# Storing attention's rows: 32 whole rows per transfer from all 128 partitions instead of quarter rows from 32 partitions

## The chip, the core and the metric

The kernel runs on one core of one Trainium2 chip. The metric is device time in microseconds (us) of one execution. The kernel before took 713.63 us, the median of three runs (708.15, 713.63 and 713.73 us).

## The reference

The computation is an attention block whose output feeds a mixture of experts. Eight batches have eight heads each, 576 positions and 64 values per head.

```python
# attention: a coarse one over means of 4 positions, plus a local one within 3 positions
out_d = sm_attn(q_d, k_d, v_d)               # q, k, v averaged in groups of 4
out_up = np.repeat(out_d, factor, axis=2)
scores = np.where(np.abs(pos[:, None] - pos[None, :]) < factor, scale * q @ k.T, -1e9)
attn_out = out_up + softmax(scores) @ v
# rows for the experts: 4608 tokens x 512 values (8 heads x 64)
x = attn_out.transpose(0, 2, 1, 3).reshape(B * S, H * D)
logits = x @ w_gate + modality_bias[modality_id]
e_idx = argmax(logits); gate_w = softmax(logits)[e_idx]
out[mask] = gate_w * (relu(x[mask] @ w1[e]) @ w2[e])     # for each of 8 experts
```

All tensors are float32. The result has 4608 rows of 512 values.

## The kernel before

The kernel has two stages that share one instruction stream per engine. In the **attention stage** the work goes in 32 steps called pairs: a pair is two heads of one batch that lie 64 partitions apart (`tpq` to `avl`, lines 254 to 447). Four pairs make a batch. `Attention.X` (L449) adds the coarse and the local part and writes the batch's tile `X` with the 512 values of a token down four groups of 128 partitions and the tokens along the free dimension.

The **router** (`Router`, L463) works batch by batch on `X`: it computes the gate's logits (`lg` to `gt`), the place of each token in its expert's list (`pr`, `pl`), and writes the lists to the DRAM tensor `tab` with an indirect DMA from GpSimd (`scatter`, L600). Two more steps bring the tokens' rows to DRAM, so that the experts can gather them:

- `R` (L580) transposes 128 tokens at a time on VectorE, in blocks of 32 by 32. After it, partition 32 a + j of tile `R` holds, for block i of 32 tokens, the 128 values with number 128 a to 128 a + 127 of token 32 i + j. These 128 values (512 bytes) lie side by side, as do the blocks i of one partition. One tile `R` takes two transposes, so 256 tokens in 8 blocks, or 128 tokens where a batch has an odd number of tiles.
- `store` (L590) copies one such tile to the DRAM tensor `xs`, which has one row of 512 values (2 KB) per token. This is what the change touches.

A batch has 576 tokens, so two batches fill nine tiles of 128: even batches handle four tiles in two stores, odd batches five tiles in three stores.

The order of the instructions is written out by hand. `PHASE` (L55) gives each step its due time, counted in pairs; `build` makes a list of calls with those times, sorts it, and issues them in that order under a manual schedule (L1115 to L1132). The stores `W0`, `W1` and `W2` are due 9.1, 11.1 and 8.5 pairs after the first pair of their batch. All plain DMAs are issued by SyncE (SP), and so stand in one queue in that order: the loads of q and k (`load_qk`, L221, three buffers each, due about four and a half pairs ahead of use), the loads of v (`load_v`, L233, two buffers), the stores, the lists of the first two units of expert work (`entries`, L826), and the weights (`wload`, L788, four buffers).

GpSimd has its own queue, in which steps of attention (`halves`, `whole`, `nl`, `nd`) stand with three kinds of work for the experts that are interleaved into the last batches: the scatter of the lists, the gather of rows for the first two units (`gather`, L844, the indirect DMA of L858, which reads `xs` and needs the unit's list `tg`), and the rounding of the first weights (`wsplit`, L800, L815 and L821), which waits for the weight load `raw`.

The **expert stage** begins inside the last pairs. A unit of work is up to 512 tokens of one expert; each product is made of three matmuls on rounded parts (`compute`, L888, line 906; `second`, L939, line 954). The first two units take tokens of the first four batches alone, so their rows can be gathered while attention goes on. The last batch's steps are issued in the stretch where the stages meet (L1140 to L1154): its row tiles go out by `R` and `store`, the last one through a tile named `o`.

Of the kernel before, what the change touches and what calls it, by code (L numbers as in the profile page):

```python
# [462 lines left out]
class Router:  # L463
# [126 lines left out]
    def store(s, b, t):  # L590

        n = min(2, s.t["G", b] - 2 * t)
        if n > 0:
            r0 = 128 * (s.t["t0", b] + 2 * t)
            R = s.t.pop(("R", b, t))
            for a in range(4):
                s.nc.sync.dma_start(s.xs[r0 : r0 + 128 * n, 128 * a : 128 * a + 128].rearrange("(i j) x -> j i x", j=32),
                                    R[32 * a : 32 * a + 32, : 4 * n].rearrange("p i k c -> p i (k c)"))

    def scatter(s, t0, t1):  # L600
        nc, C = s.nc, s.C
# [659 lines left out]
```

## Time and profile before

| | |
|---|---|
| median of three runs | 713.63 us (708.15 to 713.73) |
| the profiled execution, its own time | 717.73 us |
| its span, first to last instruction | 716.0 us |
| mean granted TensorE clock | 0.974 |
| attention stage | to about 275 us of the span |
| expert stage | from about 273 us to the end |
| stores of rows (L597) | 80 DMAs, issued from 77.8 to 285.3 us |

Busy time, idle time and waits come from the one profiled execution, and times in it count from the span's start. PE is TensorE's matmuls, PEld its weight loads, DVE is VectorE, ACT is ScalarE, POOL is GpSimd, and SP is SyncE, which issues the plain DMAs (SPq). A row of a timeline gives start, length, engine, line, operation, output and inputs, how many instructions were merged, and in brackets the idle time before the first one with what ended it. The "DMA share" is the mean busy share of the core's 16 DMA engines. A "packet" is one piece moved by one of them.

### The profile page before, as it was taken

Reading aid. Unit: us, or ns where it says so; the run is one execution under the profiler, and the core shown is the slowest. Engines: PE = TensorE matmul, PEld = TensorE weight load, DVE = VectorE, ACT = ScalarE, POOL = GpSimd, SP = SyncE. Lnnn points to the kernel's source line nnn. Section 1 sums busy time; section 2 is a strip of 40 time slices with the busy share of each in tenths; the row PEclk is TensorE's granted clock in tenths of the full one; section 3 lists DMA queues with packets and bytes.
Section 4 is the critical chain, followed back from the end, with each engine's and each line's share of the span. In section 5 each row is a group of like instructions: output and inputs, shape, how many; then the busy total and the mean of one; then the engine's idle time right before and its main releaser. Section 6 shows DMA issues by size and latency. Waiting matters only on the chain. (4 is left out here: it accounts for less than half of the span.)

```text
span 716.0 us, 19629 instructions
## 1 busy us (share of the span) xinstructions
PE 661.5 (92%) x7659; PEld 530.3 (74%) x7659; DVE 380.6 (53%) x877; ACT 359.1 (50%) x804; POOL 274.0 (38%) x366
## 2 busy tenths in 40 slices
PE   7889999998987689899999999999999999999894
PEld 4667676766765566787888888888888888889793
DVE  3678687797857585845732435224342343426610
ACT  4678777876855473634442344324443243425610
POOL 6746665856647658155030220401204012210211
PEclk9899999999998999999999999999999999999998
DMA  9799886997979767649562652535614345245600
GB/s 180 149 183 180 157 184 145 152 197 146 167 143 197 138 173 153 185 160 316 145 186 78 162 191 67 168 118 148 206 54 127 144 133 176 62 130 174 206 21 29
DMA packets 179584, 107.94 MB, mean 151 GB/s; under 512 B 139452, under 2 KB 157922, under 8 KB 179490
## 3 DMA queue, kind: packets, MB, share of 16 engines
q1 hardware_dynamic: 172274, 87.49, 52.7%
q0 software_dynamic: 7216, 19.18, 8.2%
q8 instruction: 61, 1.00, 0.7%
q14 instruction: 33, 0.27, 0.1%
HBM read 87.39 MB, written 19.51 MB: 149 GB/s over the span
## 5 line engine op out<-in xcount | busy, mean ns | idle before, releaser
L821 DVE TENSOR_TENSOR wlo<-raw,whi 128x1024 fp32r<-128x1024 f32 x73 | 87.6, 1224 | 87.0 <-ACT whi L815 66.6
L965 POOL DMA_INDIRECT out_dram<-o,tg x33 | 37.0, 1122 | 233.7 <-ACT o L957 179.7
L911 DVE SCALAR_TENSOR_TENSOR hl<-l,hh 128x512 fp32r<-128x512 f32 x72 | 49.4, 689 | 103.5 <-ACT hh L910 101.4
L954 PE MATMUL l<-whi,hh 128*128 128x512 f32 x256 | 100.5, 396 | 2.5 <-ACT hh L935 2.5
L954 PE MATMUL l<-whi,hl 128*128 128x512 f32 x256 | 99.8, 390 | 0.0
L954 PE MATMUL l<-wlo,hh 128*128 128x512 f32 x256 | 99.7, 390 | 0.0
L906 PE MATMUL l<-xh,whi 128*128 128x512 f32 (+1 forms) x256 | 95.7, 377 | 3.3 <-DVE hl L911 1.8
L910 ACT ACTIVATE hh<-l 128x512 fp32r<-128x512 f32 x72 | 42.8, 597 | 110.0 <-PE l L906 109.0
L906 PE MATMUL l<-xh,wlo 128*128 128x512 f32 (+1 forms) x256 | 94.8, 370 | 0.0
L906 PE MATMUL l<-xl,whi 128*128 128x512 f32 (+1 forms) x256 | 94.8, 370 | 0.0
L815 ACT CAST whi<-raw 128x1024 fp32r<-128x1024 f32 x70 | 71.5, 1050 | 31.3 <-DMA raw<-in_moe_w_dram 17.0
L957 ACT ACTIVATE o<-l,tg 128x512 f32<-128x512 f32 x37 | 25.3, 687 | 99.1 <-PE l L954 71.1
L906 PEld LDWEIGHTS l<-xh,whi 128*128 128x128 f32 x256 | 48.5, 190 | 12.8 <-DVE hl L911 2.1
L407 ACT COPY Pw<-lt 32x288 f32<-32x288 f32 x128 | 54.6, 427 | 6.6 <-issue 3.4
L954 PEld LDWEIGHTS l<-whi,hh 128*128 128x128 f32 x256 | 48.2, 188 | 12.2 <-ACT hh L935 2.7
L954 PEld LDWEIGHTS l<-wlo,hh 128*128 128x128 f32 x256 | 48.1, 188 | 10.1
L954 PEld LDWEIGHTS l<-whi,hl 128*128 128x128 f32 x256 | 48.3, 189 | 9.5
L337 PE MATMUL sc<-kT,qT 64*24 64x32 f32 x3072 | 45.4, 195 | 10.5 <-issue 9.6
L906 PEld LDWEIGHTS l<-xh,wlo 128*128 128x128 f32 x256 | 48.2, 188 | 8.3
L906 PEld LDWEIGHTS l<-xl,whi 128*128 128x128 f32 x256 | 48.3, 189 | 8.1 <-issue 0.2
L337 PEld LDWEIGHTS sc<-kT,qT 64*24 64x24 f32 x3072 | 35.2, 101 | 24.5 <-issue 20.2
L391 POOL TENSOR_TENSOR le<-le,zr 128x384 f32<-128x384 f32 x32 | 26.7, 835 | 63.9 <-DVE zr L387 56.4
(244 smaller groups left out, 1283.2 us busy)
## 6 DMA issues: line engine op xcount, KB each, us to landing
raw<-in_moe_w_dram SPq DMA_DIRECT2D x176, 128.0 KB
raw<-in_moe_w_dram SPq DMA_DIRECT2D x44, 512.0 KB
vw<-in_v_dram SPq DMA_DIRECT2D x53, 192.0 KB
qt<-in_q_dram SPq DMA_DIRECT2D x30, 288.0 KB
kt<-in_k_dram SPq DMA_DIRECT2D x30, 288.0 KB
xs<-R SPq DMA_DIRECT2D x64, 128.0 KB
vw<-in_v_dram SPq DMA_DIRECT2D x15, 96.0 KB
xs<-R SPq DMA_DIRECT2D x12, 64.0 KB
```

The costliest lines, as they stand in the source:

```text
L337: s.nc.tensor.matmul(p[32 * j : 32 * j + SUB, i, :], qT[r, q0 : q0 + SUB], kT[r, q0 : q0 + WIN], start=False, stop=(i == NB - 1), skip_gro ...
L391: s.nc.gpsimd.tensor_tensor(e, e, z[:, : 2 * NB].unsqueeze(2).broadcast_to([128, 2 * NB, WIN]), op=ALU.mult)
L407: s.nc.scalar.copy(s.Pw[n % NPW][r, :, j, :SUB], s.t["lt", n][r, :, :SUB])
L815: (nc.gpsimd.tensor_copy if turn <= 4 else nc.scalar.copy)(hi, raw)
L821: (nc.gpsimd if turn == 4 else nc.vector).tensor_tensor(lo, raw, hi.bitcast(F32), op=ALU.subtract)
L906: nc.tensor.matmul(p[:, f % n, :], a[:, fs], x[:, k, :N], start=(k == 0 and i == 0), stop=(k == 3 and i == 2))
L910: nc.scalar.activation(hh[:, g, :N], p, AF.Relu)
L911: nc.vector.scalar_tensor_tensor(hl[:, g, :N], p, 0.0, hh[:, g, :N].bitcast(F32), op0=ALU.max, op1=ALU.subtract)
L954: nc.tensor.matmul(p, a[:, f, hs], x[:, f % 2, :], start=(f == 0 and i == 0), stop=(f == 7 and i == 2))
L957: nc.scalar.mul(o, p, T[:, h, 1:2].bitcast(F32))
L965: nc.gpsimd.indirect_dma_start(out=s.out[:, :], out_offset=bass.IndirectOffsetOnAxis(ap=T[:, h, 0:1], axis=0), in_=o, in_offset=None, boun ...
```

## The change

`store` issues other transfers for the same bytes. Before, a tile went out in four DMAs, one for each quarter a of the 512 values: each read 32 partitions and all blocks of the tile, and wrote a quarter (512 bytes) of 256 rows (of 128 rows for a tile of one transpose). After, a tile goes out in one DMA for each block i of 32 tokens, so eight of them (or four): each reads 512 bytes from all 128 partitions and writes 32 whole rows. Written as access patterns, outermost dimension first, a DMA's DRAM side was (j: 32, i: 8, x: 128 values) and its SBUF side (partition: 32, i: 8, 128 values); now the DRAM side is (a: 4, j: 32, x: 128 values) and the SBUF side (partition: 128, 128 values). The pieces that lie side by side on both ends are 512 bytes long in both kernels. Nothing else differs.

```diff
             r0 = 128 * (s.t["t0", b] + 2 * t)
             R = s.t.pop(("R", b, t))
-            for a in range(4):
-                s.nc.sync.dma_start(s.xs[r0 : r0 + 128 * n, 128 * a : 128 * a + 128].rearrange("(i j) x -> j i x", j=32),
-                                    R[32 * a : 32 * a + 32, : 4 * n].rearrange("p i k c -> p i (k c)"))
+            for i in range(4 * n):
+                s.nc.sync.dma_start(s.xs[r0 + 32 * i : r0 + 32 * i + 32].rearrange("j (a x) -> a j x", a=4),
+                                    R[:, i].rearrange("p k c -> p (k c)"))
```

## The prediction

> **What bounds the kernel now.** I read the page first, then stretches of the span, then the queues that the change touches.
>
> ```profile
> span 716.0 us, 19629 instructions
> PE 661.5 (92%) x7659; PEld 530.3 (74%) x7659; DVE 380.6 (53%) x877; ACT 359.1 (50%) x804; POOL 274.0 (38%) x366
> DMA  9799886997979767649562652535614345245600
> q1 hardware_dynamic: 172274, 87.49, 52.7%
> ```
>
> TensorE is busy 92% of the span, but the DMA digits (40 slices of 17.9 us) say that the first 13 slices are another regime: there the 16 DMA engines are busy six to nine tenths of the time. The table by stretches separates the stages; its last three columns are the granted clock, the DMA share and GB/s.
>
> ```profile
> 50.00:60.00 10.00, 10.00 (x272) 7.64 (x272) 7.77 (x25) 8.41 (x29) 5.27 (x9) 1.00 0.99 201
> 78.00:236.00 158.00, 140.21 (x3433) 105.24 (x3428) 117.92 (x368) 112.53 (x342) 101.47 (x146) 0.96 0.87 166
> 78.00:283.00 205.00, 178.46 (x4062) 133.02 (x4058) 148.87 (x448) 138.13 (x418) 133.08 (x178) 0.95 0.83 162
> 290.00:716.00 426.00, 410.42 (x1962) 343.31 (x1960) 175.34 (x251) 164.53 (x225) 88.65 (x86) 0.99 0.46 140
> ```
>
> After 290 us TensorE is busy for 410.4 of 426 us with DMA at 0.46: a delay at the stage's start passes to the end nearly whole. From 78 to 236 us, where stores and attention's loads run together, TensorE leads (140.2 of 158 us), yet the DMA engines are at 0.87. They have 0.13 x 158 = 20.5 us free, each. That is the margin which the change draws on.
>
> SP's timeline, and three waits of other engines for what SP issues:
>
> ```profile
> 66.92 3.39 SPq L230 DMA_DIRECT2D kt<-in_k_dram  x2
> 70.37 7.36 SPq L250 DMA_DIRECT2D vw<-in_v_dram  x4
> 77.82 4.05 SPq L597 DMA_DIRECT2D xs<-R  x4
> 81.97 3.45 SPq L230 DMA_DIRECT2D qt<-in_q_dram  x2
> ...
> 91.00 0.60 PE L274 MATMUL tp<-ident,qt 128*128 128x128 f32 x4
> ...
> 212.79 1.08 POOL L858 DMA_INDIRECT xg<-xs,tg  x1 [6.38 <-DMA xs<-R]
> 215.21 0.84 POOL L391 TENSOR_TENSOR le<-le,zr 128x384 f32<-128x384 f32 x1
> 242.59 1.04 POOL L815 CAST whi<-raw 128x1024 fp32r<-128x1024 f32 x1 [5.68 <-DMA raw<-in_moe_w_dram]
> 283.19 0.71 DVE L588 STREAM_TRANSPOSE o<-X 128x512 f32<-128x512 f32 x1 [4.38 <-DMA xs<-R]
> 283.83 1.27 DVE L911 SCALAR_TENSOR_TENSOR hl<-l,hh 128x512 fp32r<-128x512 f32 x2
> ```
>
> SP goes from a load to a store to a load without a pause, and the q and k issued by 70.3 us are first used at 91.0 us, so loads run 20 us ahead of TensorE. POOL and DVE have no such cover: POOL already sits 6.38 and 5.68 us for a landing, with attention's L391 right behind, and DVE 4.38 us for a store, with the experts' first L911 behind it.
>
> **How many DMA engines a store uses.** I call the DMAs of one tile a store. The four DMAs of one store of 256 rows ran almost alone from 262 to 270 us; a stretch with loads alone is 50 to 60 us. The q1 row of the DMA view for each, in that order:
>
> ```profile
> q1 hardware_dynamic: 1088, 0.52, 24.5%
> ```
>
> ```profile
> q1 hardware_dynamic: 7835, 1.97, 97.9%
> ```
>
> Four DMAs of 128 KB are 4 x 256 = 1024 packets of 512 bytes; the 64 others are 16 per DMA, which I read as one completion from each engine that takes part. So each is spread over 16 engines, and the store takes 24.5% of 8 us, 1.96 us, on each. Loads take 0.979 x 160 us / 7835 = 20.0 ns per packet.
>
> Does every DMA use 16? The view of issues holds 25 rows of SP, 463 DMAs; the first, the last and those that matter:
>
> ```profile
> raw<-in_moe_w_dram SPq DMA_DIRECT2D x176, 128.0 KB
> xs<-R SPq DMA_DIRECT2D x64, 128.0 KB
> xs<-R SPq DMA_DIRECT2D x12, 64.0 KB
> xs<-o SPq DMA_DIRECT2D x4, 64.0 KB
> R<-in_moe_modality_id_dram SPq DMA_DIRECT2D x1, 36.0 KB
> vw<-in_v_dram SPq DMA_DIRECT2D x1, 7.2 KB
> vw<-in_v_dram SPq DMA_DIRECT2D x1, 6.8 KB
> tg<-tab SPq DMA_DIRECT2D x1, 1.0 KB
> ```
>
> Their KB over the row length in the code give 122,872 packets of q, k and v (256 bytes), 18,432 of stores, 16,896 of weights and 6,692 of small transfers: 164,892. The page's queue row has 172,274, so 7,382 are completions. 463 x 16 would be 7,408; 26 are missing. Three DMAs have an outermost count that 16 doesn't divide: the 36.0 KB one (36 rows of 1 KB), the 7.2 KB one (29 rows of 256 bytes) and the 6.8 KB one (27 rows). Were each run on the largest number up to 16 that divides its count, 12, 1 and 9 engines, then 4 + 15 + 7 = 26 are missing, exactly. I take that as the rule for SP's DMAs here, with the largest common divisor of the two ends' outermost counts. The store's ends were 32 and 32, so 16 engines. After the change they are 128 partitions and a = 4: **four engines**.
>
> The Trainium skill states this rule too (DMA: Bandwidth & Descriptors, "Why a DMA increments its semaphore by 16 and not by 1": the largest k up to 16 that divides both slowest dimensions), and adds that on this path the lowest-numbered k are used, which no row here shows; the trace agrees on the divisor by those 26 packets. By a flat sixteen engines the sum would be the third case below.
>
> **The change part by part.** *Removed and added DMAs.* Each of the 64 DMAs of 128 KB becomes two of 64 KB; the 16 of 64 KB stay as many.
>
> ```profile
> L597 SPq DMA_DIRECT2D xs<-R x76: 302/461/4037, 77.8 to 283.2; - x76
> ```
>
> 64 more issues at the median of 461 ns are 29.5 us of SP's time (19.3 at the minimum of 302). Up to 236 us there are 40 of them, 18.4 us, under the 20 us by which loads run ahead; and where engines are late SP waits for them anyway. I cost it at nothing in the forecast; its bare price is the third case.
>
> *Moved packets.* Their number and size stay, but a store of 256 rows now takes 4 x 1.96 = 7.84 us on four engines: 5.88 us more on those four, nothing on the other twelve. All loads run on 16 engines, so each is as late as its share on the four. Stores issued before 236 us and before 280 us:
>
> ```profile
> xs<-R SPq DMA_DIRECT2D x40, 128.0 KB
> xs<-R SPq DMA_DIRECT2D x8, 64.0 KB
> ```
>
> ```profile
> xs<-R SPq DMA_DIRECT2D x60, 128.0 KB
> xs<-R SPq DMA_DIRECT2D x12, 64.0 KB
> ```
>
> That is 10 + 1 = 11 and 15 + 1.5 = 16.5 stores of 256 rows. By 236 us the four engines have 11 x 5.88 = 64.7 us more to do, and 20.5 free: 44 us late, if packets stay as slow as in this stretch. If they go at the pace of the calmer rows, the stretch's 166 GB/s x 158 us = 26.2 MB, less 5.8 MB of stores, are 79,900 load packets; at 20.0 ns over 16 engines 99.9 us, with 11 x 7.84 = 86.2 together 186 us: **28 us late**. I take 28, since twelve engines then stand idle for much of the time and have little to crowd the four.
>
> *Who waits.* The queue behind a store holds the next q, k, v (cover 20 us), the list `tg` that POOL's gather needs at 212.79 and the weights that POOL's cast needs at 242.59. These two have no cover, so attention's L391 behind them is late by the queue's lag: 28 us at the cast; the gather's smaller share is contained in it.
>
> *The end of attention.* SP's rows show two stores 4.5 us apart, whose landing DVE's transpose seems to await at 283.19:
>
> ```profile
> 273.13 6.38 SPq L597 DMA_DIRECT2D xs<-R  x8
> ...
> 277.66 1.85 SPq L597 DMA_DIRECT2D xs<-R  x4
> ```
>
> At 7.84 us each the second ends 15.7 us after 273.13 instead of 277.66 + 1.96 - 273.13 = 6.5 after it: 9 us more, in front of L911 and so of the experts' first unit. Stores after that have TensorE's first unit to hide them.
>
> Sum: 28 + 9 = **37 us**. With the slow packets and no gap in the four engines' work until 283 us it is 16.5 x 5.88 - 0.17 x 205 = 62 us. With the 20 us of cover taken in full against the 28 it is 8 + 9 = 17.
>
> The profiled execution would go from 717.73 to 755 us. It stood 4.1 us above the median of 713.63; from the median, 37 more are **751 us**.
>
> **The rivals.** *Four engines, but covered.* POOL's two waits find other cover and only loads count: 17 us, 731 us, down to 722 with half of that. For it speaks the 20 us lead, against it the 6.38 and 5.68 us in front of L391.
>
> *Still spread over 16 engines*, or over another four each time, so that the change only cuts transfers smaller. Then SP's issues remain: nothing while covered, and after 273 us eight more, 3.7 us, in front of DVE's wait: 714 to 718 us. Against it stand the 26 packets.
>
> *Faster.* On 16 engines again, pieces of 64 KB land sooner, and POOL's 6.38 and DVE's 4.38 us go: 713.6 - 10.8 = 703 us. It decides only if a store's own landing, not the list behind it, ends those waits, and if 16 engines stay. The last DMA of a tile is issued later than before, which speaks against it.
>
> **How the numbers follow.** Forecast 0.70 (own range 735 to 776, that is 62 us more), covered 0.16, spread 0.10, faster 0.04. About 1% (706.5 to 720.8 us) is what a measurement can tell from no change. Slower 0.85: the first two cases, less the covered one's edge. Same 0.11, faster 0.04. The range leaves out spread and faster below and, above, the tail past the 62 us: 722 to 778 us.
>
> **What would show it.** In the profile after, the completions in q1 tell the engines: 144 DMAs with four (576) in place of 80 with 16 (1280) leave 172,274 - 704 = 171,570 packets; with 16 each (2304) there would be 173,298. The DMA share from 78 to 236 us would fall although the bytes are the same, POOL's waits before L858 and L815 grow from 6 us to 20 or more, and L906 starts some 30 us later, with the stretch after it as long as before. With 171,570 packets and the time within 1%, the cover is wrong; with 173,298, the rule is.

## The result and the profile after

| | before | after |
|---|---|---|
| median, on the same chip | 710.89 us (708.13 to 713.73) | 749.64 us (748.11 to 752.3) |
| ratio after / before, 95% interval | | 1.0541 (1.0484 to 1.0597) |
| profiled execution, its span | 717.73 us, 716.0 us | 749.11 us, 747.4 us |
| mean granted TensorE clock | 0.974 | 0.949 |

The change costs 38.75 us of median. The head of the page after, with the row of SP's queue:

```profile
span 747.4 us, 19728 instructions
PE 666.1 (89%) x7659; PEld 533.6 (71%) x7659; DVE 382.9 (51%) x877; ACT 358.7 (48%) x804; POOL 271.1 (36%) x366
DMA  9799776767688555485956163461634524344700
...
q1 hardware_dynamic: 171570, 87.49, 49.4%
```

TensorE runs the same 7659 matmuls (666.1 us busy against 661.5); its share fell because the span grew. The queue row has 171,570 packets, to the packet what the prediction gave for four engines. Digits 14 to 16 of the DMA row fell from 7 6 7 to 5 5 5.

The profile of before that the prediction was made on ran its attention stage late. A second profile of before, taken with the experiments (time 706.7 us), has everything from attention's last pairs on 8 to 11 us earlier: POOL's first weight cast at 233.89 us instead of 242.59, the end at 705.0 instead of 716.0. Its time is near the medians of before (706 to 711 us), so single times are compared with it from here on; against the first profile the lags come out some 10 us smaller. Its head, its stretch of stores and loads (the columns are as in the prediction), POOL's two waits, DVE's wait, and ACT's fourth weight cast of the first unit:

```profile
span 705.0 us, 19629 instructions
...
q1 hardware_dynamic: 172274, 87.49, 52.5%
```

```profile
78.00:236.00 158.00, 140.33 (x3570) 106.56 (x3566) 119.81 (x372) 115.86 (x353) 102.30 (x146) 0.97 0.90 175
```

```profile
204.42 1.07 POOL L858 DMA_INDIRECT xg<-xs,tg  x1 [0.68 <-DMA xs<-R]
233.89 1.04 POOL L815 CAST whi<-raw 128x1024 fp32r<-128x1024 f32 x1 [4.01 <-DMA raw<-in_moe_w_dram]
272.53 0.71 DVE L588 STREAM_TRANSPOSE o<-X 128x512 f32<-128x512 f32 x1 [3.91 <-DMA xs<-R]
284.11 1.05 ACT L815 CAST whi<-raw 128x1024 fp32r<-128x1024 f32 x1 [4.22 <-DMA raw<-in_moe_w_dram]
```

The same of after, the table by stretches first, then the timelines:

```profile
78.00:236.00 158.00, 127.71 (x3093) 96.41 (x3090) 109.81 (x341) 102.39 (x314) 89.63 (x130) 0.91 0.72 145
315.00:318.00 3.00, 3.00 (x24) 2.56 (x24) 2.04 (x17) 0.38 (x1) 0.63 (x1) 1.00 0.29 87
```

```profile
201.10 1.09 PE L274 MATMUL tp<-ident,qt 128*128 128x128 f32 x4 [3.18 <-DMA qt<-in_q_dram]
205.12 1.09 PE L274 MATMUL tp<-ident,kt 128*128 128x128 f32 x4 [2.94 <-DMA kt<-in_k_dram]
...
226.09 1.07 POOL L858 DMA_INDIRECT xg<-xs,tg  x1 [12.65 <-DMA xs<-R]
...
261.46 1.04 POOL L815 CAST whi<-raw 128x1024 fp32r<-128x1024 f32 x1 [11.31 <-DMA raw<-in_moe_w_dram]
...
304.15 0.71 DVE L588 STREAM_TRANSPOSE o<-X 128x512 f32<-128x512 f32 x1 [7.26 <-DMA xs<-R]
...
325.53 1.04 ACT L815 CAST whi<-raw 128x1024 fp32r<-128x1024 f32 x1 [10.15 <-DMA raw<-in_moe_w_dram]
```

By the two sets of rows the cast is 27.6 us later than in the second profile of before, DVE's `o` 31.6, ACT's fourth cast 41.4 and the end 42.4. A profile of the changed kernel on another chip (**r_after** below) has the same four at 261.33, 302.83, 325.55 and 744.4 us. All of the loss is there by the first unit's weights; from ACT's fourth cast on, after takes 421.9 us and before 420.9. At 201 and 205 us TensorE itself waits for q and k: the 20 us lead of the loads is used up.

SP's last stores of after, and one stretch in the middle of attention:

```profile
149.85 3.95 SPq L597 DMA_DIRECT2D xs<-R  x6
153.91 2.27 SPq L230 DMA_DIRECT2D qt<-in_q_dram  x2
156.27 2.42 SPq L230 DMA_DIRECT2D kt<-in_k_dram  x2
158.74 4.81 SPq L250 DMA_DIRECT2D vw<-in_v_dram  x4
163.65 7.86 SPq L597 DMA_DIRECT2D xs<-R  x8
...
293.91 21.16 SPq L597 DMA_DIRECT2D xs<-R  x20
315.18 2.84 SPq L597 DMA_DIRECT2D xs<-o  x4
318.28 0.45 SPq L796 DMA_DIRECT2D raw<-in_moe_w_dram  x1
```

In the first five rows SP goes from group to group with 0.05 to 0.11 us between them, as it did before. The stores are nearly alone from 315 to 318 us, and the DMA engines are then busy to 0.29 with 87 GB/s: about a quarter of the 16, as four engines would be. The first unit's weight load stands behind them, at 318.28; in the second profile of before it is this row:

```profile
274.41 2.37 SPq L597 DMA_DIRECT2D xs<-o  x4
277.03 0.40 SPq L796 DMA_DIRECT2D raw<-in_moe_w_dram  x1
```

How long SP takes to issue one store DMA, before (second profile) and after, as minimum, median and maximum in ns:

```profile
L597 SPq DMA_DIRECT2D xs<-R x76: 303/478/1956, 75.9 to 273.8; - x76
```

```profile
L597 SPq DMA_DIRECT2D xs<-R x140: 503/630/2562, 75.8 to 314.2; - x140
```

### The profile page after: what moved, and what is told of

Read it like the earlier page. It is cut to its first block, busy times and chain, and to the rows that moved or that the text cites. A ratio compares the mean times of both kernels' runs of the same rounds, so it can differ in the third digit from the quotient of the medians.

```text
span 747.4 us, 19728 instructions
## 1 busy us (share of the span) xinstructions
PE 666.1 (89%) x7659; PEld 533.6 (71%) x7659; DVE 382.9 (51%) x877; ACT 358.7 (48%) x804; POOL 271.1 (36%) x366
## 3 DMA queue, kind: packets, MB, share of 16 engines
q1 hardware_dynamic: 171570, 87.49, 49.4%
## 5 line engine op out<-in xcount | busy, mean ns | idle before, releaser
L965 POOL DMA_INDIRECT out_dram<-o,tg x33 | 35.5, 1076 | 253.1 <-ACT o L957 196.2
L954 PEld LDWEIGHTS l<-whi,hh 128*128 128x128 f32 x256 | 48.7, 190 | 18.4 <-DVE hl L911 6.3
L337 PEld LDWEIGHTS sc<-kT,qT 64*24 64x24 f32 x3072 | 33.7, 101 | 15.9 <-issue 11.3
L603 POOL DMA_INDIRECT tab<-ig,si x36 | 38.1, 1059 | 19.1 <-DVE mbase L738 12.9
```

Of the source, the lines that this page charges most:

```text
L337: s.nc.tensor.matmul(p[32 * j : 32 * j + SUB, i, :], qT[r, q0 : q0 + SUB], kT[r, q0 : q0 + WIN], start=False, stop=(i == NB - 1), skip_gro ...
L603: i = nc.gpsimd.indirect_dma_start(out=s.tab[:, :], out_offset=bass.IndirectOffsetOnAxis(ap=C.si[:, t : t + 1], axis=0), in_=C.ig[:, t, :] ...
L954: nc.tensor.matmul(p, a[:, f, hs], x[:, f % 2, :], start=(f == 0 and i == 0), stop=(f == 7 and i == 2))
L965: nc.gpsimd.indirect_dma_start(out=s.out[:, :], out_offset=bass.IndirectOffsetOnAxis(ap=T[:, h, 0:1], axis=0), in_=o, in_offset=None, boun ...
```

## The experiments

Each ratio is against the kernel before on the same chip. Unless said otherwise an experiment is an edit of the kernel before.

### The engines: 64 KB DMAs on sixteen, and odd cuts of the partitions

**e1** makes the change's 144 DMAs of 64 KB, but from 32 partitions each, so that 16 divides both outermost counts.

```diff
-            for a in range(4):
-                s.nc.sync.dma_start(s.xs[r0 : r0 + 128 * n, 128 * a : 128 * a + 128].rearrange("(i j) x -> j i x", j=32),
-                                    R[32 * a : 32 * a + 32, : 4 * n].rearrange("p i k c -> p i (k c)"))
+            for i in range(0, 4 * n, 4):
+                for a in range(4):
+                    r = r0 + 32 * i
+                    s.nc.sync.dma_start(s.xs[r : r + 128, 128 * a : 128 * a + 128].rearrange("(i j) x -> j i x", j=32),
+                                        R[32 * a : 32 * a + 32, i : i + 4].rearrange("p i k c -> p i (k c)"))
```

> The same 144 DMAs of 64 KB as in the changed kernel, but each reads 32 partitions and half of a tile's blocks, so that both ends have an outermost count of 32. Theory (a DMA runs on the largest number up to 16 that divides both outermost counts, and four engines are what cost the time): 16 engines again, q1 holds 173,298 packets, and the time is that of before, 711 us, to about 4 more. Rival (more and smaller transfers cost SP's time and the queue's): about 749, as with the change. Rival (whole rows are slower to write than quarter rows): 711 too, so this run does not tell that one from the theory.

Measured: 731.11 us against 706.13, ratio 1.0333 (1.025 to 1.0415). The page's row, and SP's timeline at the end of the stores:

```profile
q1 hardware_dynamic: 173298, 87.50, 50.9%
```

```profile
285.56 11.85 SPq L599 DMA_DIRECT2D xs<-R  x20
297.51 1.89 SPq L599 DMA_DIRECT2D xs<-o  x4
299.65 0.40 SPq L798 DMA_DIRECT2D raw<-in_moe_w_dram  x1
```

With 173,298 packets all 144 DMAs ran on sixteen engines, and the time still rose by 25.0 us. More than half of the change's loss is thus not a matter of four engines. Issuing the last 24 store DMAs, in the changed kernel 24.11 us from the first to the end, takes 13.84 here.

**e2** and **e3** keep the old form and cut each DMA in two by partitions: 31 and 1, or 24 and 8. By the rule of the prediction they run on 1 and 1, or on 12 and 8 engines.

```diff
+                dst = s.xs[r0 : r0 + 128 * n, 128 * a : 128 * a + 128].rearrange("(i j) x -> j i x", j=32)
+                src = R[32 * a : 32 * a + 32, : 4 * n].rearrange("p i k c -> p i (k c)")
+                for j0, j1 in ((0, 31), (31, 32)):     # e3: ((0, 24), (24, 32))
+                    s.nc.sync.dma_start(dst[j0:j1], src[j0:j1])
```

> Each transfer of before is cut in two, of 31 and of 1 partitions: quarter rows as before, 160 DMAs, and only the outermost counts differ. Theory: 31 has no divisor up to 16 but 1, so every store runs on one engine. A store of 256 rows takes 16 x 1.96 = 31.4 us there, 29.4 more, and 18 stores 530 more. The change made 18 x 5.88 = 106 us of such work and cost 38.7, so 67 found room; 530 - 67 is 460 more, about 1,170 us, and q1 holds 172,274 - 1,280 + 160 = 171,154 packets. Rival (number and size of the DMAs): 711 to 750 us. Rival (whole rows are slower to write): 711 to 715 us.

> As the cut into 31 and 1 partitions, with 24 and 8 instead: again 160 DMAs. Theory: 12 and 8 engines, so the first eight engines have 24 packets per quarter where they had 16, 1.5 x 1.96 = 2.94 us per store. That is 0.98 more, 18 us in the whole stage, less than the 67 that found room: 711 to 714 us, with 172,274 - 1,280 + 80 x 20 = 172,594 packets in q1. Rival (number of DMAs): 740 to 760 us, since there are more of them than with the change.

Measured: e2 1051.29 us in a single run (before: 706.13); e3 723.9 us, ratio 1.0245 (1.0185 to 1.0306), between what the theory and the rival expected: 80 more DMAs on 12 and 8 engines cost 17.8 us. The pages' rows, e2 first, with its stretch of stores and loads:

```profile
q1 hardware_dynamic: 171650, 87.49, 34.6%
```

```profile
78.00:236.00 158.00, 86.15 (x1874) 63.47 (x1874) 63.09 (x202) 61.40 (x191) 52.94 (x77) 0.73 0.33 68
```

```profile
q1 hardware_dynamic: 172594, 87.49, 51.1%
```

e3's 172,594 is exact (80 DMAs with 12 and 80 with 8 completions in place of 80 with 16: 172,274 - 1,280 + 1,600). e2 has 496 more than the rule as I had put it. The 80 DMAs of one partition account for them: if the count that matters is the outermost one that isn't 1, theirs is the number of blocks, 8 in 64 DMAs and 4 in 16, and 172,274 - 1,280 + 80 x 1 + 64 x 8 + 16 x 4 = 171,650, exactly. The Trainium skill words it so (DMA: Bandwidth & Descriptors, "Why a DMA increments its semaphore by 16 and not by 1": the slowest dimension that isn't of size 1); the trace agrees, by these 496. e2 also shows what the rule can cost: with 31 of 32 partitions on one engine, the DMA share is 0.33 and TensorE works 86 of 158 us. And it shows that a store's issuing time on SP is no fixed price. Its minimum, median and maximum in ns are here:

```profile
L600 SPq DMA_DIRECT2D xs<-R x152: 247/1608/8022, 76.1 to 611.1; - x152
```

Before, with one partition more in each DMA and sixteen engines, the median was 478 and the maximum 1956.

### Where along the attention stage

**e5** makes the change for the stores of the first six batches alone, **e6** for the last two alone, and **r_after** is the changed kernel again, on another chip.

```diff
+            if b < B - 2:        # e6: b >= B - 2
+                for i in range(4 * n):
+                    s.nc.sync.dma_start(s.xs[r0 + 32 * i : r0 + 32 * i + 32].rearrange("j (a x) -> a j x", a=4),
+                                        R[:, i].rearrange("p k c -> p (k c)"))
+            else:
+                for a in range(4):
...
```

> The change for the first six batches alone; the last two are stored as before. Theory (the four engines fall behind over the stage, and GpSimd passes the lag to attention): GpSimd's first cast is late by 19 us as in the changed kernel, and the stores after it add nothing, so 17 to 22 us more than before, 728 to 733 us. Rival (early lag is absorbed and the crowd of stores at the end makes the time): 711 to 719 us.

> The change for the last two batches alone; the first six are stored as before. In the changed kernel's trace the weights behind the last stores were late by 10 us more than GpSimd's cast, and TensorE waited 5.94 us for what they feed. Theory (the last stores, on four engines, hold up those weights whether or not attention was late): 9 to 15 us more than before, ratio 1.013 to 1.021. Rival (that wait exists only on top of the earlier lag): 1.00 to 1.008.

> The changed kernel again, beside before on the chip of the next two. Its ratio was 1.054 (1.048 to 1.060). The cut into 144 DMAs on 16 engines cost 1.033 (1.025 to 1.042) on another chip, so the number of DMAs seems to hold most of the loss, and four engines the rest, some 2% or 14 us. Both theories expect 1.05 here again, 743 to 750 us where before takes 706 to 711.

Measured: e5 728.33 us, 1.033 (1.027 to 1.039); e6 716.8 us, 1.012 (1.0073 to 1.0168); the change again 745.28 us, 1.0527 (1.0488 to 1.0566). The two parts add up to 4.5%, against 5.3 or 5.4% for the whole, a difference within the intervals. e6 shows the price of the last stores by itself: 1.2% of 707.56, 8.5 us, a little under what its theory expected. In e5, POOL's first weight cast:

```profile
255.46 1.04 POOL L820 CAST whi<-raw 128x1024 fp32r<-128x1024 f32 x1 [10.10 <-DMA raw<-in_moe_w_dram]
```

It stands 21.6 us behind that of the second profile of before, close to e5's whole loss of 22.2 us (728.33 - 706.13): what the early stores cost is there by POOL's cast and stays.

### The number of DMAs by itself

**e9** has e1's 144 DMAs, but issues a tile's second half (`h` = 1, 128 rows, four DMAs) half a pair later, behind the next loads of q and k.

```diff
-    def store(s, b, t):
+    def store(s, b, t, h=0):
...
+                        if f == "W":
+                            call(4 * b + p + 0.5, ro.store, b, i, 1)
```

> The same 144 DMAs of 64 KB on 16 engines as in the run that cut each transfer in halves by blocks, but a tile's second four are issued half a pair later, behind the next loads of q and k, so that no more than four stores follow each other. Theory A (each DMA costs SP about 0.5 us of issue, and SP has no time left): the same as without the split, 1.025 to 1.04, 725 to 735 us. Theory B (SP keeps at most eight DMAs in flight, since each waits for the landing of the eighth before it; eight small ones in a row let the queue run dry): the loss goes, 1.00 to 1.012, up to 717 us.

Measured: 721.71 us, 1.0202 (1.0168 to 1.0236). This is less than theory A expected and more than theory B. Against e1, on another chip, some 1.3% come back, so part of the loss seems to hang on eight store DMAs standing in a row; the larger part stays.

**e12** leaves the old stores and puts one DMA of 1 KB behind each of the 64 large ones, a piece of 64 bytes from each of 16 partitions, into a DRAM tensor that nothing reads. The number of DMAs grows as in the change, the bytes by 0.07 MB.

```diff
+                if n == 2:
+                    s.nc.sync.dma_start(s.junk[s.nj], R[32 * a : 32 * a + 16, 0, 0, 0:16])
+                    s.nj += 1
```

> The kernel before, with a transfer of 1 KB (16 partitions of 64 bytes, to a DRAM tensor that nothing reads) behind each of the 64 DMAs of 128 KB. SP issues 144 DMAs, eight in a row, as with the change, but rows go out in the old DMAs and the 64 others move next to nothing. Theory (the count of DMAs costs, by SP's issue and by its limit of eight in flight, not their size or engines): as the cut into halves, ratio 1.025 to 1.04, 725 to 735 us. Rival (smaller pieces are moved less well): 1.00 to 1.01.

Measured: 727.55 us, 1.031 (1.0257 to 1.0364). 64 DMAs that move nothing worth the name cost 20.4 us (from 707.15), about as much as e1's 64. The page's rows, and the issuing time of the tiny DMAs (minimum, median, maximum in ns):

```profile
span 722.5 us, 19717 instructions
...
q1 hardware_dynamic: 174322, 87.56, 51.4%
```

```profile
L600 SPq DMA_DIRECT2D junk<-R x64: 313/448/3024, 74.8 to 298.1; - x64
```

The packets are 64 x (16 pieces + 16 completions) more than before. The 16 engines are no busier over the whole run: 0.514 x 722.5 = 371 us each, against 0.525 x 705.0 = 370 in the second profile of before. The two theories of e9, SP's issuing time and the limit of eight DMAs in flight, are told apart by SP's waits. In e12, from 77 to 236 us, these name a landing of an earlier DMA (us in total, times, longest):

```profile
SPq L600 <- DMA vw<-in_v_dram: 0.8, 1, 0.8
SPq L230 <- DMA junk<-R: 0.5, 1, 0.5
SPq L597 <- DMA vw<-in_v_dram: 0.2, 1, 0.2
```

That is 1.5 us; in e1 the same view has 0.4 us and in the changed kernel none. Waiting for the eighth DMA before is thus not what costs the 20.4 or 25.0 us. In that stretch the DMA engines are also less busy than before, not more: 0.90 in the second profile of before, 0.80 in e12 and 0.79 in e1, whose row is

```profile
78.00:236.00 158.00, 131.82 (x3162) 98.51 (x3160) 112.42 (x351) 104.89 (x321) 92.15 (x132) 0.91 0.79 153
```

What is left is SP's issuing: 64 x 448 ns = 28.7 us of its time, of which 20.4 show in the result.

**e10** goes the other way: tiles of 512 tokens in two buffers, and 48 store DMAs in place of 80. A batch's first 256 tokens so wait for the next 256, and go out two pairs later than before (11.1 in place of 9.1).

```diff
-                                        s.rp.tile([128, 8, 4, 32], F32, name="R", bufs=s.nr))
+                                        s.rp.tile([128, 4, 4, 32], F32, name="R4", bufs=1) if t == 4 else
+                                        s.rp.tile([128, 16, 4, 32], F32, name="R", bufs=s.nr))
...
-        n = min(2, s.t["G", b] - 2 * t)
+        n = min(4, s.t["G", b] - 4 * t)
```

> The other direction: quarter rows from 32 partitions as before, but from tiles of 512 tokens, so 48 DMAs (32 of 256 KB, 16 of 64 KB) instead of 80; two such tiles take the room of the four. If the number of store DMAs costs 0.3 to 0.4 us each, 32 fewer give 10 us: ratio 0.985 to 0.99, 696 to 701 us where before takes 706 to 711, and the first kernel that beats both. If SP's time is only short where stores come eight in a row, nothing: 0.995 to 1.005. If the later stores of 512 tokens hold up the tile, 1.005 to 1.02.

Measured: 707.42 us, 1.0009 (0.9966 to 1.0052): no gain. Whether the later stores ate up one is not separated. Issuing one of these larger DMAs takes longer:

```profile
L598 SPq DMA_DIRECT2D xs<-R x44: 303/754/2312, 87.7 to 274.0; - x44
```

48 x 754 ns are 36.2 us, 80 x 478 ns of before are 38.2: SP's time for the stores hardly fell. By pieces per DMA the median issue is 448 ns for 16 (e12), 444 for 128 (e1), 478 for 256 (before) and 754 for 512: level up to 256, and dearer beyond. Why, the row doesn't say.

### POOL's two waits

**b0** is the kernel before again, for its second profile (rows above). **e7** puts POOL's gather two pairs later and its weight casts one pair later in the changed kernel, **e8** does the same in the kernel before.

```diff
-                call(t + 4.75 + 0.3 * i, rows, 0, i)
+                call(t + 6.75 + 0.3 * i, rows, 0, i)
...
-                    call(w + 1.5 + 0.6 * c + 0.25 * j, wsplit, c)
+                    call(w + 2.5 + 0.6 * c + 0.25 * j, wsplit, c)
```

> The kernel before again, for a second profile. The one shown at the start took 717.73 us, where the median of all its runs since is 706 to 711, and the run that changes the last two batches alone, which is the kernel before up to 260 us, has GpSimd's gather at 201.28 and its first cast at 228.97 us, not at 212.79 and 242.59. If that profile was an unusually slow one, this one takes 704 to 712 us with the gather near 201 and the cast near 229, and the change's lag at the cast is about 32 us instead of 19. If it was usual, the gather and the cast come again at 213 and 243.

> The changed kernel with two steps of GpSimd's queue due later: the gather for the first unit by two pairs, the rounding of the first weights by one. In its trace GpSimd stands 12.65 us before that gather and 11.31 us before that cast, with attention's L391 behind it. Theory (these two waits, which have no cover, hand the queue's lag to attention, but the last stores and the weights behind them come when they come): 5 to 15 us less than the changed kernel, ratio to before 1.03 to 1.045. Rival (loads of q, k and v are as late by then, so attention waits for them instead): unchanged, 1.048 to 1.057.

> The same two steps due later in the kernel before, as a candidate to beat both. If GpSimd's waits of 6.38 and 5.68 us in the trace of before are there in usual runs, up to 10 us less: ratio 0.985 to 0.995. If they belong to that one slow profile, no change: 0.996 to 1.004.

Measured: e7 748.1 us, 1.0591 (1.0529 to 1.0652), no better than the change; e8 705.68 us, 0.9974 (0.9941 to 1.0008). e7's rows of POOL and of DVE's `o`:

```profile
235.56 1.06 POOL L858 DMA_INDIRECT xg<-xs,tg  x1 [0.16 <-issue]
...
262.66 1.04 POOL L815 CAST whi<-raw 128x1024 fp32r<-128x1024 f32 x1 [7.94 <-DMA raw<-in_moe_w_dram]
...
304.61 0.71 DVE L588 STREAM_TRANSPOSE o<-X 128x512 f32<-128x512 f32 x1 [9.30 <-DMA xs<-R]
```

The gather's 12.65 us wait is gone, the cast's is down to 7.94, and `o` comes when it came in the changed kernel (304.61 against 304.15 us). POOL's waits show the lag of SP's queue; they are not the only way by which it reaches the end: at 201 and 205 us TensorE waits for q and k itself.

## Why the prediction was right or wrong

Predicted 751 us, measured 749.64; 37 us more, measured 38.75. That the number came so near is in good part luck: the issues, costed at nothing, and the four engines, costed too high, are two errors that offset.

**How many engines a store uses: right.** The q1 counts follow to the packet: 171,570 after, 173,298 in e1, 172,594 in e3, and 171,650 in e2 once a dimension of size 1 is passed over.

**"I cost it at nothing": the step that failed.** The 64 more issues, priced at 29.5 us of SP's time and then written off against the 20 us by which loads run ahead, cost 25.0 us in e1 and 20.4 in e12, where no four engines are in play. Two things were overlooked. A lead of 20 us is a stock, used up once; by the prediction's own 18.4 us the issues up to 236 us alone use nearly all of it, and it was wanted by the four engines too. And the argument's other half, "where engines are late SP waits for them anyway", needs pauses that more issues can fill. SP has hardly any: of the 159 us from 77 to 236 the groups of SP's timeline (short gaps within a group included) fill 151 in the second profile of before and 153 in e1 and after. With the same time filled, SP issued 89 DMAs that are not stores before, 74 in e1 and 70 after. The rows were there to read; "without a pause" should have become "is full". How much of each issue is SP's own work and how much a hold-up by the engines these rows don't say; e2's 1608 ns suggest that there can be such a hold-up.

The Trainium skill says that the time a sequencer needs to initiate a DMA "is usually small relative to the DMA itself" (DMA: Bandwidth & Descriptors, "Issuing engines are not separate DMA queues"). Against the engines' time it is not small here: a median of 0.45 to 0.63 us, for 64 KB that keep sixteen engines busy for 0.25 us (an eighth of the prediction's 1.96 us for 512 KB).

**The queue's lag of 28 us at POOL's cast: right in size, wrong in make-up.** The cast is 27.6 us late by the rows above (18.9 against the first profile, which was itself late). In e1 it is late already by 20.0:

```profile
253.93 1.04 POOL L817 CAST whi<-raw 128x1024 fp32r<-128x1024 f32 x1 [8.66 <-DMA raw<-in_moe_w_dram]
```

So what comes with four engines adds 7.5 us there, where I had given them 28. The mis-sized term is the 7.84 us for a store on four engines. From 315 to 318 us the stores moved 87 GB/s, so 512 KB take 524,288 / 87,000 = 6.0 us. That is at most what four engines need: SP issues a DMA of 64 KB every 0.71 us there (2.84 us for four), which is 92 GB/s, and so may set the pace itself. In the prediction's own sum eleven such stores are 66 us in place of 86; with the 99.9 us of loads that makes 166 in a stretch of 158, 8 us late at most, where the runs show 7.5. How near these two are is not to be leaned on, since SP's lag had thinned the loads of that stretch already.

**POOL's two waits "have no cover": right as a sign, not as the cause.** They grew from 0.68 and 4.01 us to 12.65 and 11.31, short of the 20 that the prediction gave as its sign, but e7 takes most of the first away and gains nothing: q, k and v are late by then as well.

**The end of attention, 9 us: too large, and in the wrong place.** From the cast to `o` before took 38.6 us, after 42.7: 4.1 us, not 9. The sentence **"Stores after that have TensorE's first unit to hide them" failed**: 24 store DMAs of 64 KB stand in front of the first unit's remaining weights, and ACT's fourth cast, 11.6 us after `o` before, comes 21.4 us after it, 9.8 more. In e1, with as many on sixteen engines, it is not late:

```profile
291.85 0.71 DVE L588 STREAM_TRANSPOSE o<-X 128x512 f32<-128x512 f32 x1 [2.49 <-DMA xs<-R]
...
304.19 1.05 ACT L817 CAST whi<-raw 128x1024 fp32r<-128x1024 f32 x1 [3.07 <-DMA raw<-in_moe_w_dram]
```

12.3 us after `o`, as against 11.6 before. That is where the change's own shape does hurt, by four engines or by its longer issues (see below), and e6, which has only the late stores in the changed form (16 more DMAs among them), shows it too:

```profile
270.19 0.71 DVE L588 STREAM_TRANSPOSE o<-X 128x512 f32<-128x512 f32 x1 [5.12 <-DMA xs<-R]
...
290.58 1.04 ACT L820 CAST whi<-raw 128x1024 fp32r<-128x1024 f32 x1 [8.76 <-DMA raw<-in_moe_w_dram]
```

The cast comes 20.4 us after `o`; e6's whole loss is 1.2%.

**What the two causes are worth.** By medians the count of DMAs costs 3.1 to 3.3% (e12, e1), four engines, with all that comes with this shape, the other 2% or so: 5.3% of the repeat less e1's 3.3, on different chips, so 1 to 3% with the intervals. By the profiles of before (second), e1 and after, ACT's fourth cast goes from 284.11 to 304.19 to 325.53 us, 20.1 and 21.3 more; the span from 705.0 to 728.1 to 747.4 us, 23.1 and 19.3 more:

```profile
span 728.1 us, 19728 instructions
```

The profiles are single executions on different chips, so the medians' 2% is the safer figure for four engines.

**The rivals.** "Four engines, but covered" at 731 falls. "Still spread over 16 engines" falls on the packet count, but its price for the issues alone (nothing while covered, 714 to 718) is refuted by e1, which is that case built: 731.11. "Faster" asked for smaller pieces on sixteen engines, which e1 has, and came out 25 us slower. From ACT's fourth cast on, the kernel takes as long as before, 421.9 against 420.9 us, as the prediction said of the stretch after the first units.

**What stays open.** A store DMA's issue takes 303 ns at least on sixteen engines and 503 on four, 200 ns more, and I have not separated this from the four engines' own transfer time: both come with the shape, and 144 x 0.2 = 29 us is enough to matter. Nor is it settled how much of e12's and e1's loss is bare issuing and how much is SP held up within an issue; waits for landings are ruled out above, and e9's 1.3% suggests only that the order counts. Part of the loss also shows as a slower TensorE and not as waiting: from 78 to 236 us its granted clock is 0.97 in the second profile of before and 0.91 in e1 and after, and the same 7659 matmuls keep it busy for 654.6, 662.7 and 666.1 us by the pages. Whether the lower clock follows from the waits or adds to them no run here tells. No version tried is clearly faster than the kernel before.

## What to carry to other kernels

Read an issuing queue as an engine: add up its issue rows over the stretch, and where they fill it, price each further DMA (here 0.2 to 0.4 us each in e9, e3, e12 and e1, whatever its bytes), while a lead of loads is a stock to be spent once. Before reshaping a transfer, work out its engines from the outermost counts of both ends, passing over those of 1: 16 should divide them, and the queue's packet row tells whether it does. Stores at a stage's end stand in front of the next stage's loads on the same queue; price them at that load's first user.

## What the hardware showed that was not expected

- 64 DMAs of 1 KB on a full SP queue cost 3.1% (2.6 to 3.6), as much as splitting 64 DMAs of 128 KB in two (3.3%, 2.5 to 4.2), at the same busy time of the DMA engines (371 and 370 us each in e12 and before).
- Fewer and larger ones gave nothing back: 48 DMAs in place of 80 came to 1.0009 (0.9966 to 1.0052), with the median issue up from 478 to 754 ns.
- A DMA of one partition is spread by its next dimension (8 or 4 blocks), one of 31 partitions sits on one engine, and with the stores in that form the kernel took 1051.29 us.
- The least issue time of a store DMA with the same 128 pieces of 512 bytes was 302 ns on sixteen engines (e1) and 503 on four (after):

```profile
L599 SPq DMA_DIRECT2D xs<-R x140: 302/444/3582, 75.4 to 297.1; - x140
```
